# Strided scores of batch 1 in one half-array run, batch 0's strided x transposed before its last local scores: an attention and MLP kernel on one core

## The chip, the cores and the metric

The kernel runs on one core of a Trainium2 chip. The metric is the device time of one execution in microseconds. Five engines run beside each other, each through its own instruction list in order, and wait for each other through semaphores: TensorE (PE: matmuls and transposes; PEld is its loading of weights), VectorE (DVE), ScalarE (ACT), GpSimd (POOL) and SyncE (SP), which only issues DMA transfers here. Matmul results land in PSUM, eight banks of 2 KB per partition; VectorE and ScalarE copy them from there into SBUF.

## What is computed

```python
scores = scale * np.matmul(q, k.transpose(0, 1, 3, 2))          # B=8, H=8, S=576, D=64
mask_local = (rel >= 0) & (rel < 32)                            # heads 0 to 3
mask_strided = (rel >= 0) & (pos[None, :] % 32 == pos[:, None] % 32)   # heads 4 to 7
attn = softmax(np.where(masks, scores, -1e9))
x = (attn @ v).transpose(0, 2, 1, 3).reshape(B * S, H * D)      # 4608 x 512
h = x @ w_in                                                    # 512 -> 2048
out = (h * np.tanh(softplus(h))) @ w_out                        # 2048 -> 512
```

All inputs and the output are float32; the matmuls work in bf16.

## The kernel before

The 4608 rows of x are worked on in nine blocks of 512. For a block t there are two projections: `mlp1` (x times w_in, then Mish on ScalarE) and a second product (times w_out, then the store). Batch 1's attention is threaded into block 0's second product, batch 2's into block 1's, and so on. The order of all instructions is written out by hand; no scheduler changes it.

Strided attention (kind "s") of a batch is sixteen score tiles of 72x72, one for each of 4 heads and 4 pairs of residues; local attention (kind "l") is six windows of 96 queries and 128 keys for four heads. Both are cut into three parts ("s", 0) to ("s", 2) and ("l", 0) to ("l", 2). The steps are:

- `t_step` transposes a batch's q or k on PE (line 253 strided, line 267 local) and copies the result to qTs, kTs, qTl or kTl. The local transposes use 64 of the array's 128 columns.
- `qk` (line 333) computes one part's scores. Its contraction is over 64 rows, half of the array. An exp on ScalarE (line 347) follows. For batch 0 the mask is added before by `bias` (line 304); for later batches `mask` (line 353) multiplies the exps by 0 or 1.
- `pv` (line 369) multiplies the exps by v and a column of ones, and VectorE divides by the sum: a reciprocal and a multiplication (lines 380 and 381) into x_s or x_l. `pv2` (lines 394 and 395) does two at once. A step V of kind s, number i, is called "V s i" below, of kind l "V l i".
- `xt` transposes x_s (line 418) or x_l (line 408) and copies it into xT, the input of the first projection. `xt_now` and `xt_later` do the same for x_l window by window, the first on PE, the second by a transposing DMA in SyncE's queue.

Run here means a stretch of half-array matmuls with full-array matmuls before and after it. A half-array run is made either by `qk` or by a local `t_step`.

PSUM is handed out as three accumulators of two banks (`acc(i)`, i = 0 to 2, one buffer each) and two single banks that `tile_t` hands out in turn (the pool tag is "pt"). A new tile in a buffer waits until the last reader of the former tile is done.

Batch 0's attention (lines 904 to 958) stands before everything else: there is no projection yet to hide it. Its strided scores, local transposes, local scores, outputs and transposes of x are written one after another, then block 0's first projection. That projection's first three groups are split in two halves: `g1s` needs only the strided half of xT (four w_in matmuls a group, 128x512, line 522), the other halves also the local part.

Block 0's second product has sixteen steps of four matmuls (line 781, 128x512 each). Step i is followed by the list `at[i]` of batch 1's attention steps (`attn_steps`, the branch with x == y, lines 455 to 474) and by a few more that lines 966 to 977 append: loads for batch 2, sums of w_out's quarters (line 656) and the transposing DMAs for batch 2. The steps use w_out in four parts, each loaded by a DMA of its own; steps 8 to 11 need the third. After step 15 block 1 begins with line 553 (psu).

Of the kernel before, what the change touches and what calls it, by code (L numbers as in the profile page):

```python
# [11 lines left out]
BF16 = mybir.dt.bfloat16  # L12
# [5 lines left out]
WQ = 96  # L18
CL, PL = 6, 96
# [24 lines left out]
def kernel(ctx, tc, q, k, v, moe_w_in, moe_w_out, out):  # L44
    nc = tc.nc
    B, H, S, D = q.shape
# [87 lines left out]
    def by_head(x):  # L134

        return x[0:PL].rearrange("p j h d -> p (j h d)").rearrange("p (h x) -> p h x", h=4)
# [19 lines left out]
    def spread_v_str(b, eng):  # L156
        cast(eng, vs[b % 2][0:PN, :, :, 0:D], vs_raw().rearrange("p h (j d) -> p h j d", d=D))
# [37 lines left out]
    def cast(eng, out_, in_):  # L195
        if eng is nc.scalar:
            nc.scalar.copy(out_, in_)  # L197
        else:
            eng.tensor_copy(out_, in_)
# [42 lines left out]
            eng.memset(vl[b % 2][0:32, 0, :, 0:D], 0.0)  # L242


    def t_step(b, kind, which, hp, eng=None):

        eng = eng or nc.vector
        tr = tile_t("tr")[:].bitcast(BF16)
        if kind == "s":
            src = (qs if which == "q" else ks)[b % 2]  # L250
            for u in range(8):
                h, jj = 2 * hp + u // 4, u % 4
                nc.tensor.transpose(  # L253
                    tr[:, PN * u:PN * u + PN],
                    src[0:PN, h, 128 * jj:128 * jj + 128],
                    ident[0:PN, 0:PN],
                )
            dst = (qTs if which == "q" else kTs)[:, 8 * SU * hp:8 * SU * hp + 8 * SU]
            cast(
                eng, dst.rearrange("c (u n) -> c u n", u=8)[:, :, 0:PN],  # L260
                tr[:, 0:S].rearrange("c (u n) -> c u n", u=8),
            )
        else:
            src = by_head((ql if which == "q" else kl)[b % 2])
            for j in range(CL):
                for e in range(2):
                    nc.tensor.transpose(  # L267
                        tr[64 * e:64 * e + 64, PL * j:PL * j + PL],
                        src[:, 2 * hp + e, D * j:D * j + D], ident[0:PL, 0:PL],
                    )  # L270
            dst = qTl[:, hp, :] if which == "q" else kTl[:, hp, 32:32 + S]
            cast(
                eng, dst.rearrange("c (p j) -> c p j", j=CL),
                tr[:, 0:S].rearrange("c (j p) -> c p j", j=CL),
            )

    def unread(n, i_acc=None):

# [15 lines left out]
    class Attn:  # L294
# [129 lines left out]
                    tr[:, 0:576].rearrange("p (j n) -> p n j", j=CS),  # L424
                )

        def xt_now(self, n):
            tr = tile_t("trx")[:].bitcast(BF16)
            t0 = (self.b % RING) * S
            for c in range(2):  # L430
                for w in range(n):
                    o = (n * c + w) * WQ
                    nc.tensor.transpose(
                        tr[:, o:o + WQ], x_l[0:WQ, w, 128 * c:128 * c + 128], ident[0:WQ, 0:WQ]
                    )
            cast(
                nc.scalar, xT[:, 0:2, t0:t0 + n * WQ],
                tr[:, 0:2 * n * WQ].rearrange("p (c n) -> p c n", c=2),
            )

# [6 lines left out]
    def attn_steps(b, x, y):  # L447

        a = Attn(b)
        Q = lambda i_acc, *parts: (lambda: a.qk(parts, i_acc))  # L450
        M = lambda kd, i: (lambda: a.mask(kd, i, nc.vector))
        V = lambda kd, i: (lambda: a.pv(kd, i))
        X = lambda kd, hf: (lambda: a.xt(kd, hf))
        s0, s1, sl2, l0, l1 = ("s", 0), ("s", 1), (("s", 2), ("l", 2)), ("l", 0), ("l", 1)
        if x == y:
            T = [(lambda n=n, eng=eng: t_step(b, *T_ORDER[n], eng)) for n, eng in enumerate(
                (None, None, None, None, None, nc.scalar, None, nc.scalar))]
            return [
                T[2:4], [Q(x, s0)],
                [M(*s0), Q(x, s1)],  # L460
                [lambda: spread_v_str(b, nc.vector), V("s", 0)],
                [V("s", 1), M(*s1), Q(x, ("s", 2))],
                [V("s", 2), T[4]],
                [V("s", 3), M("s", 2), T[5]],
                [V("s", 4), T[6]],
                [V("s", 5), T[7]],
                [V("s", 6), Q(x, l0)],
                [V("s", 7), M(*l0), Q(x, l1)],
                [X("s", 0), V("l", 0), M(*l1), Q(x, ("l", 2))],
                [X("s", 1), V("l", 1), M("l", 2)],  # L470
                [V("l", 2), V("l", 3)],
                [V("l", 4), V("l", 5)],
                [lambda hf=hf: a.xt("l", hf, nc.vector) for hf in range(2)],
            ], T[0:2]
        V2 = lambda kd, i, z: (lambda: a.pv2(kd, i, z))
        G = lambda kd, i: (lambda: a.mask(kd, i, nc.gpsimd))
        l2 = ("l", 2)
        now = -(-(512 * (b + 1) - S * b) // WQ)
        at = [
            [],  # L480
            [Q(x, s0), Q(y, s1), Q("t", *sl2), M(*s0), M(*s1), M("s", 2)],
            [],
            [V2("s", 0, y), G(*l2)],
            [],
            [V2("s", 2, y), Q(x, l0), Q("t", l1), G(*l0), G(*l1)],
            [],
            [V2("s", 4, y), lambda: nc.scalar.preload_act_table(AF.Mish)],
            [],
            [V2("s", 6, y)],
            [V2("l", 0, x)],  # L490
            [X("s", 0), V2("l", 2, y), X("s", 1)],
            [V2("l", 4, x), lambda: a.xt_now(now)],
            [lambda: a.xt_later(now)],
        ]
        return at
# [180 lines left out]
    def sums_w():  # L676

        b11, b12 = w_out[:, 0:8, 0:256], w_out[:, 0:8, 256:512]
        b21, b22 = w_out[:, 8:16, 0:256], w_out[:, 8:16, 256:512]
        return [  # L680
            lambda c: sums(tw_of(0)[:, c], b12[:, c], b11[:, c], ALU.subtract),
            lambda c: sums(tw_of(1)[:, c], b22[:, c], tw_of(0)[:, c], ALU.subtract),
            lambda c: sums(b12[:, c], b22[:, c], b12[:, c], ALU.subtract),
            lambda c: sums(tw_of(3)[:, c], b21[:, c], tw_of(1)[:, c], ALU.subtract),
        ]
# [174 lines left out]
    with tc.manual_schedule():  # L860
# [56 lines left out]
            a.qk([("s", i)], None, ps[i])  # L917
        spread_v_str(0, Dv)
        unread(3)
        t_step(0, "l", "k", 0, Dv)  # L920
        t_step(0, "l", "k", 1, Sc)
        a.qk([("s", 2)], None, ps[2])
        a.pv2("s", 0, 0)
        a.pv2("s", 2, 1)
        for hp in range(2):
            t_step(0, "l", "q", hp, Sc)
# [2 lines left out]
        a.pv2("s", 6, 1)  # L929
        a.qk([("l", 0)], None, ps[0])  # L930
        a.qk([("l", 1)], None, a.bias("l", 1, 0))
        a.qk([("l", 2)], None, a.bias("l", 2, 2))
        load_w_out(0, 1)
        load_qk_str(1)
# [5 lines left out]
        load_v_loc(1)  # L940
        accs = (1, 0, 2)
        gT, g1s, g1 = mlp1(0, accs)
        a.pv2("l", 0, 1)
        a.xt("s", 0)
        a.xt("s", 1)
        a.pv2("l", 2, 0)
        a.pv2("l", 4, 2)
        g1s[0]()
        a.xt("l", 0)
        a.xt("l", 1)  # L950
        Sc.preload_act_table(AF.Mish)
        g1s[1]()
        g1s[2]()
        for f in sums_w_in()[0:3]:
            f()
# [5 lines left out]
        for t in range(NBLK):  # L961
            if t == 0:
                x, y, z = accs
                at, ts = attn_steps(1, y, y)
                at[3] += [
                    lambda: load_early_v_str(2), lambda: load_tiles_loc(2, kl, k),
                    lambda: cast_v_loc(1, Po), lambda: load_tiles_loc(2, ql, q),
                ]
                at[12].append(lambda: transpose_by_dma(2))
                at[1].append(lambda: sums_w()[0](lo))  # L970
                at[7].append(lambda: sums_w()[0](hi))
                at[9].append(lambda: sums_w()[1](lo))
                at[11].append(lambda: sums_w()[1](hi))
                at[14].append(lambda: sums_x(1, "1"))
                at[15] += [
                    lambda: spread_v_str(2, Dv),
                ]
                out_accs = (z, x)
            else:
                if t == 1:  # L980
                    split_third()
                x, y = 0, 1
                gT, z, g1 = mlp1(t, (y, x) if t == 1 else (x, y))
                at = attn_steps(t + 1, x, y) if t + 1 < B else []
                if t == 1:
                    at[0].append(lambda: sums_w()[3](hi))
                if t + 2 < B:
                    at[10].append(lambda: transpose_by_dma(t + 2))
                if t + 1 < B:
                    at[7].append(lambda: share_v_loc(t + 1))  # L990
                if t + 2 < B:
                    at[0].append(lambda: load_qk_str(t + 2))
                if t + 1 < B:
                    at[12].append(lambda: sums_x(t + 1, "1"))
# [55 lines left out]
```

## Time and profile before

| What | us |
|---|---|
| median of 3 runs (286.89 to 287.18) | 287.12 |
| the profiled execution | 286.68 |
| its span, first to last instruction | 284.8 |
| PE's first w_in matmul (line 522) | 19.91 |
| last of 64 w_in matmuls of block 0 starts | 34.46 |
| block 0's second product: first transpose of batch 1 | 34.67 |
| block 1's first matmul (line 553) | 57.39 |
| landing of w_out's four parts | 29.47, 38.03, 46.21, 49.91 |

The profile lists one execution. A timeline line gives the start of a group of equal instructions, its busy time, the engine, the line, what it writes and reads, the shape and the count; in brackets is the idle time of the engine before it and what ended that. PE's matmuls overlap each other, so a matmul's cost is read from start to start: 0.216 us for 512 columns, 0.032 for 72.

### The profile page before, as it was taken

How to read it: one execution, taken by the hardware profiler on the slowest of the kernel's cores; microseconds unless marked ns; L12 is line 12 of the kernel's file. 1: busy time of each engine (PE TensorE's matmuls, PEld its weight loads, DVE VectorE, ACT ScalarE, POOL GpSimd, SP SyncE). 2: the span in 40 equal slices, each digit the busy share in tenths (PEclk: the TensorE clock that was granted, in tenths of full speed). 3: DMA queues.
4: the chain of work that ended last, by engine and by line, in shares of the span. 5: the costliest groups of instructions: out<-in, count | busy, mean ns of one | idle time of the engine just before them, and what ended most of it. 6: DMA issues, size and time to landing. Idle time of an engine off the chain costs nothing.

```text
span 284.8 us, 7535 instructions
## 1 busy us (share of the span) xinstructions
PE 279.0 (98%) x3121; PEld 218.6 (77%) x3121; DVE 193.0 (68%) x403; ACT 196.4 (69%) x292; POOL 106.3 (37%) x127
## 2 busy tenths in 40 slices
PE   8999999999999999999999999999999999999995
PEld 3564455586898689868988898788978997888684
DVE  2283067899877777777777778777677767644742
ACT  1578652599867987798779877987699759407820
POOL 8375534406290717271636255345404600000000
PEclk9999999999999999999999999999999999999999
DMA  7999999999989999799999999899979041003004
GB/s 155 185 202 195 190 194 201 143 145 235 169 128 129 214 173 150 139 216 158 155 138 217 122 176 136 216 135 153 157 143 164 4 154 30 0 10 140 0 2 147
DMA packets 103965, 40.73 MB, mean 143 GB/s; under 512 B 86396, under 2 KB 99436, under 8 KB 103932
## 3 DMA queue, kind: packets, MB, share of 16 engines
q1 hardware_dynamic: 67900, 25.13, 51.9%
q0 software_dynamic: 35744, 14.87, 46.8%
q8 instruction: 24, 0.39, 0.6%
q10 hardware_dynamic: 288, 0.25, 0.3%
q14 instruction: 9, 0.07, 0.1%
HBM read 37.20 MB, written 9.44 MB: 164 GB/s over the span
## 4 chain that ended last, share of the span: by engine, by line
PE 92%; DMA 2%; DVE 2%; ACT 1%; issue 0%; ACTq 0%; POOLq 0%
PE pso L748 31%; PE psu L553 10%; PE psh L522 10%; PE psv L553 9%; PE psb L553 8%; PE psb L522 5%; PE po L369 4%; PE pso L808 4%; PE pso L781 4%; PE ps L333 4%; DMA ks<-in_k_dram 2%; PE trx L418 1%; PE un L281 1%; PE tr L267 1%; PE tr L253 1%; DVE x_s L395 1%
## 5 line engine op out<-in xcount | busy, mean ns | idle before, releaser
L748 PEld LDWEIGHTS <-gT 128*128 128x128 bf16 x448 | 41.9, 98 | 5.8
L553 PEld LDWEIGHTS <-w_in 128*128 128x128 bf16 x384 | 37.4, 98 | 8.4
L353 POOL TENSOR_TENSOR Pl<-Pl,consts_sb 128x960 bf16<-128x960 bf16 (+1 forms) x18 | 29.2, 1634 | 38.2 <-issue 22.1
L748 PE MATMUL pso<-w_out,gT 128*128 128x256 bf16 x336 | 40.9, 272 | 0.0
L748 PEld LDWEIGHTS <-Sg 128*128 128x128 bf16 x336 | 31.5, 98 | 4.4
L522 PEld LDWEIGHTS <-w_in 128*128 128x128 bf16 x208 | 20.2, 98 | 16.7 <-issue 0.6
L553 PEld LDWEIGHTS <-Sw 128*128 128x128 bf16 x288 | 28.2, 98 | 3.3
L522 PE MATMUL psh<-xT,w_in 128*128 128x512 bf16 (+1 forms) x136 | 29.4, 366 | 0.2 <-ACT xT L197 0.2
L197 ACT COPY xT<-trx 128x576 bf16<-128x576 bf16 (+3 forms) x24 | 14.2, 629 | 18.4 <-PE trx L418 13.0
L748 PE MATMUL pso<-Tw,Sg 128*128 128x256 bf16 x224 | 26.7, 273 | 0.0
L197 ACT COPY osb<-pso 128x512 f32<-128x512 f32 (+1 forms) x17 | 9.4, 555 | 20.2 <-PE pso L748 10.8
L562 ACT ACTIVATE gT<-psu 128x1024 bf16<-128x1024 f32 x16 | 16.4, 1025 | 8.4 <-PE psu L553 8.4
L395 DVE TENSOR_TENSOR x_s<-po,rden 72x512 bf16<-72x512 f32 x28 | 19.2, 686 | 1.0
L656 DVE TENSOR_TENSOR psu<-psb,p 128x512 f32<-128x512 f32 x16 | 11.2, 700 | 11.8 <-PE psb L553 11.0
L533 ACT ACTIVATE gT<-psh 128x1024 bf16<-128x1024 f32 x16 | 16.2, 1024 | 4.0 <-PE psh L522 3.9
L175 POOL DMA_DIRECT2D vl<-in_v_dram x24 | 17.8, 751 | 2.0 <-issue 1.5
L656 DVE TENSOR_TENSOR Sg<-gT 128x256 bf16<-128x256 bf16 (+2 forms) x32 | 12.8, 422 | 8.0 <-ACT gT L562 6.7
L628 POOL COPY mark<-qTl 1x4 bf16<-1x4 bf16 x6 | 1.6, 268 | 44.4 <-DMA qTl<-ql 44.4
L347 ACT ACTIVATE Ps<-ps 72x864 bf16<-72x864 f32 (+1 forms) x18 | 14.7, 857 | 4.6 <-PE ps L333 4.6
L553 PE MATMUL psu<-xT,w_in 128*128 128x256 bf16 x128 | 17.9, 272 | 0.0
L725 DVE TENSOR_TENSOR p<-pso,p 128x512 f32<-128x512 f32 x14 | 9.6, 685 | 11.9 <-PE pso L748 11.9
L553 PE MATMUL psb<-Sx,w_in 128*128 128x256 bf16 x128 | 17.2, 272 | 0.0
(139 smaller groups left out, 612.8 us busy)
## 6 DMA issues: line engine op xcount, KB each, us to landing
out_dram<-osb SPq DMA_DIRECT2D x9, 512.0 KB, 3.9
out_dram<-p SPq DMA_DIRECT2D x7, 512.0 KB, 3.0
kl<-in_k_dram SPq DMA_DIRECT2D x5, 576.0 KB, 13.6
ql<-in_q_dram SPq DMA_DIRECT2D x5, 576.0 KB, 16.4
qs<-in_q_dram POOLq DMA_DIRECT2D x8, 288.0 KB, 12.0
vsr<-in_v_dram POOLq DMA_DIRECT2D x8, 288.0 KB, 9.0
w_in<-in_moe_w_in_dram POOLq DMA_DIRECT2D x4, 512.0 KB, 9.8
w_out<-in_moe_w_out_dram POOLq DMA_DIRECT2D x4, 512.0 KB, 17.9
```

The source lines that it names most:

```text
L175: nc.gpsimd.dma_start(vl[b % 2][32:128, :, h, 0:D], v[b, h].rearrange("(w p) d -> p w d", p=WQ))
L197: nc.scalar.copy(out_, in_)
L333: nc.tensor.matmul(by_e[e][:, o:o + w], lhsT=lhsT, rhs=rhs, start=not biased, stop=True, skip_group_check=biased,)
L347: nc.scalar.activation(pt[0:n, :, 0:nw], ps[0:n, :, o0:o0 + nw], AF.Exp, scale=scale)
L353: meng.tensor_tensor(out=pm, in0=pm, in1=mk[0:n, :].unsqueeze(1).unsqueeze(1).to_broadcast([n, 2, nu, w]), op=ALU.mult,)
L395: nc.vector.tensor_tensor(out=dst.rearrange("p e (h d) -> p e h d", h=4), in0=po[0:m, :, :, 0:D], in1=rden[0:m].unsqueeze(3).to_broadcast( ...
L522: nc.tensor.matmul(ps_u[:, o:o + n], lhsT=w_in[:, cc, fc * 128:(fc + 1) * 128], rhs=xT[:, cc, a:a + n], start=(cc == 2 and (o == 0 or len( ...
L533: nc.scalar.activation(to, tiles[g][:], AF.Mish)
L553: nc.tensor.matmul(p[:, 256 * j:256 * j + 256], lhsT=lhs[:, cc, f:f + 128], rhs=rhs[:, cc], start=(first and j == 0 and cc == 0), stop=(la ...
L562: nc.scalar.activation(gT[:, c:c + src.shape[1], 256 * half_t:256 * half_t + 256], src, AF.Mish,)
L656: nc.vector.tensor_tensor(out=out_, in0=in0, in1=in1, op=op)
L748: nc.tensor.matmul(ps[:, pair, :], lhsT=lhs(c, 128 * pair), rhs=rhs(c), start=(first and pair == 0 and c == 0), stop=(last and c == 7), sk ...
```

## The change

Batch 0, before the first projection:

- `pv2("s", 0)` moves ahead of the two local transposes of k, and the first of those copies goes from VectorE to ScalarE.
- The strided x is transposed (`xt("s", 0)` and `xt("s", 1)`) before the last local scores, after the first two local parts' scores; its two copies go from ScalarE to VectorE.
- Local outputs 0 and 1 are made by two single `pv` (in the two single banks) instead of one `pv2`.
- The three strided halves of the first projection no longer stand together: the first one comes after these two outputs, the second one between the transposes of local x, the third one after them.

Batch 1, inside block 0's second product:

- The two strided score parts s0 and s1 are computed in one run after step 1; s1 uses the two single banks instead of the accumulator, so its exp comes as two instructions. The spread of v and both masks follow at once on VectorE.
- The four local transposes are made in two runs instead of four, k after step 5 and q after step 7. Each pair fills one accumulator; VectorE copies its first half, ScalarE its second.
- Local x is transposed by `xt_now(5)` with one VectorE copy, its sixth window by a transposing DMA.
- One sum of w_out's quarters comes one step earlier.

```diff
+    def t_loc(b, which, hp, tr):
+        src = by_head((ql if which == "q" else kl)[b % 2])
+        for j in range(CL):
+            for e in range(2):
+                nc.tensor.transpose(
+                    tr[64 * e:64 * e + 64, PL * j:PL * j + PL],
+                    src[:, 2 * hp + e, D * j:D * j + D], ident[0:PL, 0:PL],
+                )
+        dst = qTl[:, hp, :] if which == "q" else kTl[:, hp, 32:32 + S]
+        return lambda eng: cast(
+            eng, dst.rearrange("c (p j) -> c p j", j=CL),
+            tr[:, 0:S].rearrange("c (j p) -> c p j", j=CL),
+        )
...
         if x == y:
-            T = [(lambda n=n, eng=eng: t_step(b, *T_ORDER[n], eng)) for n, eng in enumerate(
-                (None, None, None, None, None, nc.scalar, None, nc.scalar))]
+            T = [(lambda n=n: t_step(b, *T_ORDER[n])) for n in range(4)]
+
+            def t_pair(which):
+                tr = acc(x, "tr")
+                copies = [t_loc(b, which, hp, tr[:, hp, :].bitcast(BF16)) for hp in range(2)]
+                for copy, eng in zip(copies, (nc.vector, nc.scalar)):
+                    copy(eng)
+
             return [
-                T[2:4], [Q(x, s0)],
-                [M(*s0), Q(x, s1)],
-                [lambda: spread_v_str(b, nc.vector), V("s", 0)],
-                [V("s", 1), M(*s1), Q(x, ("s", 2))],
-                [V("s", 2), T[4]],
-                [V("s", 3), M("s", 2), T[5]],
-                [V("s", 4), T[6]],
-                [V("s", 5), T[7]],
+                T[2:4],
+                [Q(x, s0), Q("t", s1), lambda: spread_v_str(b, nc.vector), M(*s0), M(*s1)],
+                [],
+                [V("s", 0)],
+                [V("s", 1), Q(x, ("s", 2))],
+                [V("s", 2), M("s", 2), lambda: t_pair("k")],
+                [V("s", 3)],
+                [V("s", 4), lambda: t_pair("q")],
+                [V("s", 5)],
                 [V("s", 6), Q(x, l0)],
                 [V("s", 7), M(*l0), Q(x, l1)],
                 [X("s", 0), V("l", 0), M(*l1), Q(x, ("l", 2))],
                 [X("s", 1), V("l", 1), M("l", 2)],
                 [V("l", 2), V("l", 3)],
                 [V("l", 4), V("l", 5)],
-                [lambda hf=hf: a.xt("l", hf, nc.vector) for hf in range(2)],
+                [lambda: a.xt_now(5, nc.vector), lambda: a.xt_later(5)],
             ], T[0:2]
...
         spread_v_str(0, Dv)
         unread(3)
-        t_step(0, "l", "k", 0, Dv)
+        a.pv2("s", 0, 0)
+        t_step(0, "l", "k", 0, Sc)
         t_step(0, "l", "k", 1, Sc)
         a.qk([("s", 2)], None, ps[2])
-        a.pv2("s", 0, 0)
         a.pv2("s", 2, 1)
...
         a.qk([("l", 1)], None, a.bias("l", 1, 0))
+        a.xt("s", 0, Dv)
+        a.xt("s", 1, Dv)
         a.qk([("l", 2)], None, a.bias("l", 2, 2))
...
-        a.pv2("l", 0, 1)
-        a.xt("s", 0)
-        a.xt("s", 1)
+        a.pv("l", 0)
+        a.pv("l", 1)
+        g1s[0]()
         a.pv2("l", 2, 0)
         a.pv2("l", 4, 2)
-        g1s[0]()
         a.xt("l", 0)
+        g1s[1]()
         a.xt("l", 1)
         Sc.preload_act_table(AF.Mish)
-        g1s[1]()
         g1s[2]()
...
-                at[1].append(lambda: sums_w()[0](lo))
+                at[0].append(lambda: sums_w()[0](lo))
```

More of the change, by code (lines that the diff above doesn't have):

```diff
@@ L263, in t_step @@
         else:
[L264 to L275, printed above, removed]
+            t_loc(b, which, hp, tr)(eng)
     def unread(n, i_acc=None):
@@ L425, in xt, with xt_now @@
                 )
-        def xt_now(self, n):
+        def xt_now(self, n, eng=nc.scalar):
             tr = tile_t("trx")[:].bitcast(BF16)
@@ L436, in xt_now @@
             cast(
-                nc.scalar, xT[:, 0:2, t0:t0 + n * WQ],
+                eng, xT[:, 0:2, t0:t0 + n * WQ],
                 tr[:, 0:2 * n * WQ].rearrange("p (c n) -> p c n", c=2),
```

## The prediction

> **What bounds the kernel now.** I read the busy times first, then TensorE's waits, then the timeline of the two stretches that the diff touches.
>
> ```profile
> PE 279.0 (98%) x3121; PEld 218.6 (77%) x3121; DVE 193.0 (68%) x403; ACT 196.4 (69%) x292; POOL 106.3 (37%) x127
> ```
>
> TensorE (PE) is busy for 98% of the span, so an edit counts only by what it does to PE's start times. From 57.39 us, where block 1 begins, the matmuls stand back to back, and PE's list of waits names nothing there: whatever happens earlier shifts the end by the same amount. So I need two numbers: when PE starts the thirteenth w_in matmul (end of the prologue), and how long PE takes from there to 57.39.
>
> The prologue, in the timeline (start, duration, engine, line, tiles, count, idle before and who ended it):
>
> ```profile
> 13.47 0.76 DVE L199 COPY kTl<-tr 128x576 bf16<-128x576 bf16 x1 [1.18 <-PE tr L267]
> 13.73 0.64 ACT L197 COPY kTl<-tr 128x576 bf16<-128x576 bf16 x1
> ...
> 14.26 0.65 ACT L347 ACTIVATE Ps<-ps 72x576 bf16<-72x576 f32 x1
> ...
> 15.04 1.18 ACT L197 COPY qTl<-tr 128x576 bf16<-128x576 bf16 x2
> ...
> 17.03 0.58 PE L304 MATMUL ps<-consts_sb 128*128 128x480 bf16 x2 [0.16 <-DVE x_s L395]
> ...
> 18.85 0.20 DVE L394 RECIPROCAL rden<-po 96x8 f32<-96x8 f32 x1 [1.04 <-PE po L369]
> ...
> 20.44 0.81 PE L522 MATMUL psh<-xT,w_in 128*128 128x512 bf16 x3 [0.15 <-ACT xT L197]
> ...
> 21.72 8.58 PE L522 MATMUL psh<-xT,w_in 128*128 128x512 bf16 x39
> ```
>
> To see: PE waits for VectorE's x_s (17.03) and ScalarE's xT copies (20.44); VectorE stands idle for 1.04 us before the local outputs. From 21.72 PE runs without a gap, four w_in matmuls already done.
>
> Block 0's second product, where batch 1's attention is threaded in:
>
> ```profile
> 36.58 1.03 PE L781 MATMUL pso<-w_out,gT 128*128 128x512 bf16 x4
> ...
> 37.54 0.37 PE L333 MATMUL ps<-qTs,kTs 64*128 64x72 bf16 x12
> ...
> 37.84 1.04 PE L781 MATMUL pso<-w_out,gT 128*128 128x512 bf16 x4
> ...
> 38.95 0.37 PE L333 MATMUL ps<-qTs,kTs 64*128 64x72 bf16 x12
> ...
> 46.25 1.02 PE L781 MATMUL pso<-w_out,gT 128*128 128x512 bf16 x4
> ```
>
> To see: what a half-array run (64 rows here, 64 columns for the transposes) costs. Four 512-wide matmuls are followed by a full-array group after 0.87 us (35.19 to 36.06), by a half-array one after 0.96 (36.58 to 37.54): 0.10 to enter. Twelve half-array matmuls at 16 ns should take 0.19 us, and the next group comes after 0.30: 0.11 to leave. **A run costs 0.21 us** besides its matmuls.
>
> **Part 1, the prologue.** Hand-over times, from rows: PE's last start to a reader's start 0.24 us; ScalarE's end to PE 0.05, VectorE's 0.06; a ScalarE copy follows its neighbour after 0.54 (two in 1.18); an s pair of reciprocal and multiply takes 0.92 on VectorE. I follow the new order.
>
> ScalarE gets both k copies. pv2 s0 now leads and needs the first exp (12.15 + 0.89 = 13.04): 13.10 to 13.33 on PE. The k transposes start at 13.45, so the copies run 13.94 to 15.11 and the s2 exp 15.01 to 15.66 (before: 14.91). The q copies end at 16.74 (before: 16.22).
>
> The l0 bias goes into the accumulator that the s2 exp reads, so it waits until 15.71 (before 15.19), and in PE's queue pv2 s4 stands behind it: 16.13 (before 15.60). VectorE finishes s0 and s2 early (15.71), then idles 0.87 and does s4 until 17.51 and s6 until 18.40 (before 16.97 and 17.81). The l1 bias waits for s4: 17.57 (before 17.03); l1's scores end at 18.26, and the sixteen moved x_s transposes run 18.39 to 18.88 (0.0323 each).
>
> Their two copies are now VectorE's. The trace has no VectorE copy of this form, a read from PSUM with stride 72. The bounds are 0.46 us (VectorE's xT copies of local x, contiguous, two in 0.82 at 57.33) and 0.76 (the kTl copy at 13.47, stride 96). I take 0.75, the strided row: 18.86 to 20.28. [...]
>
> Both copies hold the two banks of the pool "pt", from which pv l0 and pv l1 now draw. Pv l1 therefore waits for the second copy: 20.36 (before, the first local outputs ran at 18.38). Behind it in PE's queue stand the first four w_in matmuls, 20.49 to 21.35, then pv2 l2 to 21.59 and l4. VectorE does l0 and l1 (0.62 each) until 21.49, l2 until 22.74, l4 until 23.64 (before: all by 21.44). The transposes of windows 0 to 2 finish at 22.94, four w_in matmuls to 23.85, the other transposes to 24.06, four more to 24.96; ScalarE's last xT copy ends at 24.94. **The thirteenth w_in matmul starts at 24.99; before, 21.72 + 8 × 0.216 = 23.45: 1.54 us later.** With copies of 0.46 the same chain gives 24.40: 0.95 later.
>
> **Part 2, block 0's second product,** on the clock of before. It took 34.67 to 57.39, 22.72 us. Removed: three runs, 3 × 0.21 = 0.62; two of twelve transposes of 42 ns, 0.08. Waits of PE that showed as late starts, 0.90 in all: s1's scores behind s0's exp on one accumulator (0.14 at 38.95); V s0 behind VectorE's spread of v (0.07); V s2 behind the s1 mask (0.14); the load of w_out (0.07 at 46.25); l1's scores behind l0's exp (0.10); V l2 to V l5 behind VectorE (0.38). s1's scores now use the pool's banks, and spread and masks come two steps earlier, so the first three go; the fourth goes because PE comes later than the landing at 46.21. **What is late next is VectorE:** from V l0 at 51.04 it has pairs, masks and a w_out sum without a break, 3.72 us to V l3's end as before (52.10 to 55.82); V l3 and V l5 wait for banks, 0.07 and 0.26, l1's scores 0.10. So 0.47 of the waits goes. Following every step, block 1 begins at 56.24 on that clock: **1.14 us saved** (the terms add up to 1.17).
>
> Costed at nothing: the w_out sum one step earlier (0.68 at 37.26, in VectorE's 0.99 of idleness before the mask); s1's exp in two halves of 72x432 (a 128x384 took 0.50, a 72x576 0.65; their mask is needed a whole step later); the pair copies, where ScalarE's waits for VectorE's in the built order (done at 44.7 and 47.1, read from 45.0 and 47.7; if that 0.3 were overrun, PE waits for the excess); VectorE's xT copy of 960 (0.46 to 0.92, done by 57.4, needed at 58.5). Window 5 goes by one transposing DMA in SyncE's queue, behind block 0's two stores and ahead of batch 3's local loads (issued at 65.30, landed 73.62 and 83.21). At 1.2 us of issue and 5.6 to landing it is there by 73; block 2 reads it after 86, the casts of the loads come after 100. POOL's order is unchanged.
>
> **Sum:** 1.54 − 1.14 = +0.40 us. The profiled execution took 286.68 us, of which 284.8 are the span and 1.9 lie around it; it becomes 287.08. It lay 0.44 below the median of 287.12, so I forecast **287.5 us**, +0.14%. About 0.2% (0.57 us) is what a measurement of this kernel can tell from no change.
>
> **Rivals.** (A, slower) VectorE takes back what the dropped runs give. Place: steps 11 to 15 of the second product, where V l2 to V l5 share two banks and VectorE has no idle time left. Price: the 0.52 us of waits and transposes are not saved, only the runs' 0.62: +0.92, 288.0. It decides as soon as VectorE reaches V l0 0.17 us later than I have it. For it: V l4 and V l5 already waited; against: VectorE reaches V l0 with 0.6 us of idleness in the trace. Chance 0.32. (B) Strided copies at the contiguous price: +0.95 − 1.14 = −0.2, 286.9, no measurable change. Against: both strided kTl copies in block 0 took 0.74. Chance 0.10. (C, faster) The prologue loses nothing, because the early transposes remove PE's 0.54 us of waiting for xT and the chain above does not bind. Then the third w_out load caps the gain: step 8 cannot start before its landing at 46.21, and only 11.13 − 10.59 = 0.54 is saved behind it (from 46.25 to 57.39 before, from 45.65 to 56.24 after): 286.6, or 286.5 if the load lands a little earlier. For it: PE's late starts in that stretch, 1.35 us in all (0.10 at 14.55, 0.28 inside the sixteen po matmuls from 15.60, 0.23 at 17.03, 0.07 at 17.93, 0.54 from 19.9 to 20.7, 0.13 inside the transposes from 21.09); against: both banks and VectorE. Chance 0.09. That the change does not do what it says is ruled out by the built order: seven runs stand there.
>
> **How the numbers follow.** Forecast 0.49, A 0.32, B 0.10, C 0.09. The forecast, B and the tamer end of C (0.02) lie within 0.2%, 0.61; slower is A, 0.32; faster the rest of C, 0.07. The range 286.8 to 288.1 takes in both copy prices (286.9 and 287.5) and A's 288.0; what is left out is C and the far side of A.
>
> **What would show it.** In the new timeline: VectorE's two xT copies of about 0.75 from 18.9; pv l1 near 20.4; the thirteenth w_in matmul near 25.0; three half-array runs fewer between there and block 1; step 8 starting past 47 without a DMA wait; block 1 at 57.8. I am wrong if ScalarE's k copies do not push the s2 exp past 15.5, if the copies take 0.46, or if V l0 to V l5 show more than 0.5 us of waits on PE.

## The result

The changed kernel takes 287.49 us (median of 22 runs, 287.25 to 288.73); the kernel before takes 286.91 us in the same series (median of 22, 286.64 to 287.52). The ratio is 1.002 with a 95% interval from 1.0014 to 1.0026: slower by 0.58 us, or 0.20%, just at the bound up to which I called it no change. Forecast was a change of +0.40 us. The profiled executions took 286.68 us (span 284.8) and 287.36 us (span 285.5).

For all that follows I cut the span into pieces that do not depend on when the inputs land. That landing differs from execution to execution: the first exp started between 12.15 and 12.89 us in the kernels measured here. The pieces are: first exp to last w_in matmul of block 0 (the prologue), from there to block 1's first matmul (the second product of block 0), and block 5, from its first matmul to block 6's.

| Piece, us | before | after | difference | forecast |
|---|---|---|---|---|
| first exp to last w_in matmul | 22.31 | 23.78 | +1.47 | +1.54 |
| last w_in matmul to block 1 | 22.93 | 21.78 | −1.15 | −1.14 |
| block 5 | 28.89 | 29.25 | +0.35 | 0 |

The other blocks agree within 0.05. The sum is +0.67, and the two profiled executions differ by 0.68. The medians differ by 0.1 less: before's profiled execution was shorter than its median (286.68 against 286.91), with inputs that landed early.

**The prologue.** First the busy times on the page of the changed kernel, then its timeline (start, duration, engine, line, tiles, shape, count, idle before and who ended it). Lines from 245 on have moved, by 3 for `qk`, `bias` and `pv`.

```profile
PE 277.5 (97%) x3104; PEld 218.4 (76%) x3119; DVE 194.2 (68%) x405; ACT 195.9 (69%) x292; POOL 106.9 (37%) x127
```

```profile
13.95 1.18 ACT L197 COPY kTl<-tr 128x576 bf16<-128x576 bf16 x2
...
15.01 0.65 ACT L350 ACTIVATE Ps<-ps 72x576 bf16<-72x576 f32 x1
...
17.55 0.58 PE L307 MATMUL ps<-consts_sb 128*128 128x480 bf16 x2 [0.42 <-DVE x_s L398]
...
18.85 1.42 DVE L199 COPY xT<-trx 128x576 bf16<-128x576 bf16 x2 [0.52 <-PE trx L421]
...
20.32 0.29 PE L372 MATMUL po<-vl,Pl 128*128 128x65 bf16 x4 [0.36 <-DVE xT L199]
...
21.77 0.20 DVE L397 RECIPROCAL rden<-po 96x8 f32<-96x8 f32 x1 [0.42 <-PE po L372]
...
22.76 0.34 PE L411 MATMUL trx<-consts_sb,x_l 96*128 96x96 bf16 x4 [0.68 <-DVE x_l L398]
```

Read against the lines of before: the s2 exp has gone from 14.26 to 15.01, behind two k copies on ScalarE; the second bias from 17.03 to 17.55, still behind VectorE's x_s; the strided copies stand on VectorE from 18.85; single output l1 waits for the second of them and starts at 20.32; and the transposes of x_l wait for VectorE until 22.76, where before they ended at 21.68. The w_in matmuls run without a break from 24.06, four of them after eight earlier ones, so the thirteenth comes at 24.92 (forecast 24.99; 23.45 before).

**The second product,** in the timeline of PE:

```profile
39.04 0.56 PE L336 MATMUL ps<-qTs,kTs 64*128 64x72 bf16 x24
...
43.80 0.70 PE L249 MATMUL tr<-consts_sb,Sg 96*64 96x96 bf16 x24
...
46.52 0.70 PE L249 MATMUL tr<-consts_sb,Sg 96*64 96x96 bf16 x24
47.15 1.04 PE L791 MATMUL pso<-w_out,gT 128*128 128x512 bf16 x4
...
57.31 0.59 PE L436 MATMUL trx<-consts_sb,x_l 96*128 96x96 bf16 x10
57.73 0.49 PE L563 MATMUL psu<-xT,w_in 128*128 128x256 bf16 x3
```

To see: s0 and s1 are one run of 24; k and q one run of 24 each; step 8 starts at 47.15 with no wait for a DMA (the third part of w_out landed at 46.23); block 1 begins at 57.73, forecast 57.8.

**Block 5** is where the forecast had nothing. The changed kernel's list of PE's waits (who waited for whom: us in total, times, longest) has a line that the list of before has not:

```profile
PE psb L563 <- DVE psu L666: 0.3, 1, 0.3
```

And the timeline of VectorE there, in the kernel before and in the changed one:

```profile
176.80 1.50 DVE L656 TENSOR_TENSOR psu<-psb,p 128x512 f32<-128x512 f32 x2 [0.24 <-PE psb L553]
```

```profile
177.17 0.70 DVE L666 TENSOR_TENSOR psu<-psb,p 128x512 f32<-128x512 f32 x1 [1.07 <-PE psb L563]
178.32 0.70 DVE L666 TENSOR_TENSOR psu<-psb,p 128x512 f32<-128x512 f32 x1 [0.46 <-PE psb L563]
```

Before, the two sums follow each other (the second 0.104 us after the first, as in every other block). In the changed kernel the second one starts 0.455 after it, though the matmuls that it is said to wait for had their last start at 177.66, 0.66 earlier; such sums otherwise start about 0.3 us after it (177.29 and 177.60 before). PE's next matmuls wait for this sum. I come to the cause below.

### The profile page after: what moved, and what is told of

Read it like the earlier page. It is cut to its first block, busy times and chain, and to the rows that moved or that the text cites. A ratio compares the mean times of both kernels' runs of the same rounds, so it can differ in the third digit from the quotient of the medians.

```text
span 285.5 us, 7520 instructions
## 1 busy us (share of the span) xinstructions
PE 277.5 (97%) x3104; PEld 218.4 (76%) x3119; DVE 194.2 (68%) x405; ACT 195.9 (69%) x292; POOL 106.9 (37%) x127
## 4 chain that ended last, share of the span: by engine, by line
PE 94%; DVE 3%; ACT 1%; issue 1%
PE pso L758 30%; PE psu L563 10%; PE psh L532 10%; PE psv L563 8%; PE psb L563 7%; PE psb L532 5%; PE po L372 5%; PE pso L818 4%; PE pso L791 4%; PE ps L336 3%; PE un L284 3%; PE trx L421 1%; PE tr L267 1%; PE ps L307 1%; PE trx L436 1%
## 5 line engine op out<-in xcount | busy, mean ns | idle before, releaser
L532 PE MATMUL psh<-xT,w_in 128*128 128x512 bf16 (+1 forms) x127 | 28.8, 366 | 0.5
L197 ACT COPY xT<-trx 128x576 bf16<-128x576 bf16 (+3 forms) x22 | 13.1, 626 | 20.9 <-PE trx L421 13.0
L350 ACT ACTIVATE Ps<-ps 72x864 bf16<-72x864 f32 (+1 forms) x17 | 13.8, 854 | 4.2 <-PE ps L336 4.2
```

The costliest lines, as they stand in the source:

```text
L350: nc.scalar.activation(pt[0:n, :, 0:nw], ps[0:n, :, o0:o0 + nw], AF.Exp, scale=scale)
L532: nc.tensor.matmul(ps_u[:, o:o + n], lhsT=w_in[:, cc, fc * 128:(fc + 1) * 128], rhs=xT[:, cc, a:a + n], start=(cc == 2 and (o == 0 or len( ...
```

## The experiments

My theory was the forecast's: two terms, each a chain worked out by hand, which add; and w_out's landing as a cap on what batch 1's part gains without batch 0's. The rivals were that the parts do not stand by themselves, that the prologue's loss has other causes than those named, and that block 5's loss belongs to one of the parts.

The results are together in this table. The pieces are those of above, in us of the profiled execution. The ratio is to the kernel before, which was measured again beside the experiments: its median was 286.96 beside batch1_only, batch0_only, pair_in_acc and k_copy_on_vector, 286.97 beside the next four rows, 286.90 beside batch1_quarters and early_xt_timed, and 286.61 (one execution) beside xt_on_scalar and early_xt_only. Differences to before are taken to these. The row early_xt is one kernel in two runs: early_xt_only, one execution of 286.14, and early_xt_timed, whose median stands there.

| Kernel | prologue | second product | block 5 | median | ratio, 95% interval |
|---|---|---|---|---|---|
| before | 22.31 | 22.93 | 28.89 | 286.91 | |
| after | 23.78 | 21.78 | 29.25 | 287.49 | 1.0020 (1.0014 to 1.0026) |
| batch1_only | 22.32 | 22.48 | 28.93 | 286.28 | 0.9978 (0.9967 to 0.9988) |
| batch0_only | 23.78 | 22.89 | 29.24 | 288.68 | 1.0062 (1.0050 to 1.0074) |
| pair_in_acc | 23.22 | 21.78 | 28.89 | 286.66 | 0.9989 (0.9980 to 0.9997) |
| k_copy_on_vector | 23.22 | 21.78 | 28.89 | 286.55 | 0.9989 (0.9980 to 0.9998) |
| after_plus_one | 23.78 | 21.78 | 28.89 | 287.32 | 1.0010 (1.0001 to 1.0019) |
| before_plus_three | 22.51 | 22.88 | 29.25 | 287.48 | 1.0011 (1.0000 to 1.0022) |
| run_added | 23.78 | 22.36 | 29.25 | 288.07 | 1.0044 (1.0027 to 1.0061) |
| batch1_halves | 22.32 | 22.04 | 28.89 | 286.01 | 0.9962 (0.9950 to 0.9975) |
| early_xt | 22.65 | 21.78 | 28.89 | 286.08 | 0.9968 (0.9954 to 0.9981) |
| xt_on_scalar | 24.04 | 21.78 | 28.89 | 287.62 (one run) | |
| batch1_quarters | 22.31 | 22.58 | 28.89 | 285.82 | 0.9959 (0.9947 to 0.9972) |

### Each part by itself

Batch 1's part alone is the changed kernel with before's lines from `spread_v_str(0, Dv)` to `g1s[2]()`. Batch 0's part alone is the changed kernel with before's `attn_steps` branch and w_out sum.

> Batch 1's part of the change alone, on the prologue of before. My theory (two terms that add, the second one capped): the second product begins at 34.67 as before; the dropped runs and waits would bring step 8 to 47.15 - 1.50 = 45.65, but it waits for the third part of w_out (46.21 before, 46.23 after) until about 46.25. The rest takes 10.58 as in the changed kernel (57.73 - 47.15), so block 1 begins at 56.8, 0.55 earlier than before, and the time is 0.55 below that of before (about 286.4). Rival 1, no cap: block 1 at 56.2, time 1.15 lower (285.8). Rival 2, the batch 1 part is what costs 0.35 us in block 5 (first projection 173.8 to 203.0 took 29.25 in the changed kernel, 28.89 before): block 5 stays 29.25 long and only 0.2 is gained.

> Batch 0's part alone, on the second product of before. My theory: the last w_in matmul of block 0 starts at 35.95 as in the changed kernel (34.46 before), +1.50; the second product is that of before without the 0.07 wait for w_out, so block 1 begins at 58.8 (57.39 + 1.50 - 0.07) and the time is 1.4 above that of before, 288.3. Rival: the 0.35 us of block 5 come from this part, then block 5 takes 29.25 and the time is 1.8 above, 288.7. If the two parts alone gave the same sum as together (+0.58), this one would have to be +1.7 with -1.15 of the other, or +1.1 with -0.55.

Batch 1's part alone gains 0.68 us in the medians, not 1.15 (0.55 was expected); in the pieces of the profiled execution its second product is 0.45 shorter. PE's timeline of that kernel shows why:

```profile
45.24 0.70 PE L249 MATMUL tr<-consts_sb,Sg 96*64 96x96 bf16 x24
46.58 1.02 PE L791 MATMUL pso<-w_out,gT 128*128 128x512 bf16 x3 [0.64 <-DMA w_out<-in_moe_w_out_dram]
```

Step 8 was due at 45.95 and waited for the third part of w_out, which landed at 46.54. From step 8 on to block 1 it took 10.58 us, the same as in the changed kernel, as expected. The cap is shown, and rivals 1 and 2 are out.

Batch 0's part alone costs 1.72 us, where my theory had 1.4 and the rival 1.8. The prologue is as expected (23.78, the same as in the changed kernel to 0.01), but block 5 is 0.35 longer here too. So this loss goes with batch 0's part. Block 5 begins over 130 us after that part has ended, which made me look for something other than a delay that is handed on.

### Block 5: a place in VectorE's instruction list

I counted the instructions in VectorE's program, waits on semaphores included, from zero. The late sum is number 320 in the changed kernel and in batch 0's part alone. It is 317 in the kernel before and in batch 1's part alone, and 318 and 321 in the two kernels below; none of these showed the gap. To test this I moved the number and nothing else, with tiny instructions where VectorE has time:

```diff
+        for _ in range(1):            # 1 in the changed kernel, 3 in the kernel before
+            Dv.memset(x_s[0:1, 0, 0:4], 0.0)
```

> The changed kernel with one more tiny VectorE instruction (a memset of four elements, written over later) among the memsets at the start. In the changed kernel and in batch 0's part alone VectorE began the second sum of block 5's second product 0.455 us after the sum before it, everywhere else 0.104 after; that instruction is number 320 in VectorE's program in these two kernels, and 317, 317, 318 and 321 in the four others measured (before and batch 1's part alone are both 317). Theory: the 0.35 us hang on the place of the instruction in VectorE's program. Then here (number 321) the gap is 0.104, block 5 takes 28.89 instead of 29.25, and the time is 0.35 below the changed kernel's: about 287.1, 0.2 above before. Rival: they hang on the time at which block 5 starts (173.8 and 175.0 in these two, 173.2 to 173.4 in the others) or on which transfers then run: the gap stays 0.455, time 287.5.

> The kernel before with three more such memsets at the start: its second sum of block 5 becomes number 320 in VectorE's program. Theory of the place: the gap there becomes 0.455, block 5 takes 29.25 instead of 28.89, time 0.35 above before. Rival (start time of block 5, or the transfers then running): nothing changes, 0.00, since block 5 starts at 173.4 as before.

VectorE's timeline in block 5, with one more instruction in the changed kernel, and then with three more in the kernel before:

```profile
177.37 1.50 DVE L666 TENSOR_TENSOR psu<-psb,p 128x512 f32<-128x512 f32 x2 [0.87 <-PE psb L563]
```

```profile
177.71 0.70 DVE L656 TENSOR_TENSOR psu<-psb,p 128x512 f32<-128x512 f32 x1 [0.63 <-PE psb L553]
178.86 0.70 DVE L656 TENSOR_TENSOR psu<-psb,p 128x512 f32<-128x512 f32 x1 [0.46 <-PE psb L553]
```

The gap went from the one and came to the other: block 5 takes 28.89 with 321 and 29.25 with 320. The start of the block does not decide: the changed kernel (start at 173.79) has the gap, the one with an instruction more (173.99) has not, the one of before with three more (174.33) has it again. The ratios moved the same way, to 1.0010 from 1.0020 and to 1.0011 from 1. The interval of the kernel with three more begins at 1.0000, and its profiled execution had a prologue 0.20 longer, for a reason that was not followed: there the trace decides, not the time. So about half of what the changed kernel loses against before is this (0.0010 of 0.0020 by the ratios, 0.35 of 0.67 us by the pieces), and it has nothing to do with what the change computes. It happened that the change makes VectorE's list three instructions longer ahead of block 5.

### The prologue's loss taken apart

Two undoings, one by one and then together. The first puts the lines around the local k transposes back; the second puts local outputs 0 and 1 into an accumulator:

```diff
-        a.pv2("s", 0, 0)
-        t_step(0, "l", "k", 0, Sc)
+        t_step(0, "l", "k", 0, Dv)
         t_step(0, "l", "k", 1, Sc)
         a.qk([("s", 2)], None, ps[2])
+        a.pv2("s", 0, 0)
```

```diff
-        a.pv("l", 0)
-        a.pv("l", 1)
-        g1s[0]()
+        a.pv2("l", 0, 1)
         a.pv2("l", 2, 0)
         a.pv2("l", 4, 2)
+        g1s[0]()
```

> The changed kernel with the lines around the local k transposes as before (first copy on VectorE, strided outputs 0 behind them). My theory (the second k copy on ScalarE delays everything behind the s2 exp by 0.52): s2 exp at 14.26, q copies end at 16.22, l0 bias 15.19, VectorE's x_s s6 until 17.81, l1 bias 17.03, xT copies 18.33 to 19.75, last w_in matmul at 35.43 instead of 35.95, block 1 at 57.2, time 0.52 below the changed kernel's, 287.0. Rival: the 0.52 us that VectorE idles ahead of its xT copies (18.33 to 18.85) absorb it, and nothing moves at the last w_in matmul: 35.95, 287.5.

> The changed kernel with local outputs 0 and 1 in accumulator 1 (one pv2, as before) and the first strided half of the projection behind all the outputs; the early transposes of x and their VectorE copies stay. My theory (the two banks that the copies hold, and the single outputs behind them, cost the largest part of the prologue's loss): the outputs run from 19.26 on, VectorE does l0 to 21.08, l2 to 21.91, l4 to 22.74 (22.70 and 23.54 for l2 and l4 in the changed kernel); the thirteenth w_in matmul at 24.3, 0.63 earlier, the last one at 35.3; step 8 at 46.5, still past the landing of w_out at 46.2; block 1 at 57.1, time 286.9, the same as before. Rival: the copies on VectorE and the later scores set the chain and the banks do not matter: last w_in matmul still within 0.1 of 35.95, time 287.5.

> Both undoings of the prologue together (k copies as before; local outputs 0 and 1 in accumulator 1, first strided half behind the outputs): of batch 0's part only the earlier transposes of strided x with their VectorE copies stay, and the place of the second strided half. Measured from the first exp to the last w_in matmul of block 0, to leave out when the inputs land: before 22.31, changed kernel 23.78, each undoing by itself 23.22. Theory: the three causes stand one behind the other in VectorE's chain and add: 23.78 - 0.56 - 0.57 = 22.65, so that the early transposes by themselves still cost 0.34. Step by step: VectorE's copies 18.33 to 19.75 and its outputs l0, l2, l4 until 20.56, 21.39, 22.22 (21.44 before), thirteenth w_in matmul at about 23.8. Rival: the early transposes cost nothing by themselves (they take PE's former wait of 0.54 for xT): 22.3 or less.

Each undoing by itself takes 0.56 or 0.57 us from the prologue (expected 0.52 and 0.63), and both together 1.13, to 22.65 as expected. In time the two single ones gained 0.94 and 0.83, not 0.52 and 0.63: both also move VectorE's instruction off number 320. So the +1.47 splits into 0.56 for the lines around the local k transposes (both copies on ScalarE, strided outputs 0 ahead of them; these two were not undone one by one, but the s2 exp stands behind the second copy in the timeline), 0.57 for the single outputs in the two banks with the w_in matmuls behind them, and 0.34 for what is left: the early transposes with their copies on VectorE, and the place of the second strided half. That the early transposes cost nothing because they free PE of its wait for xT, rival C of the forecast, is refuted: VectorE's outputs come later, and that is what PE waits for instead, as its list of waits says for the kernel with both undoings:

```profile
PE psh L532 <- DVE rden L397: 0.8, 1, 0.8
```

In that kernel VectorE has no gap from the copies to the last local output:

```profile
18.43 1.42 DVE L199 COPY xT<-trx 128x576 bf16<-128x576 bf16 x2 [0.53 <-PE trx L421]
19.77 0.19 DVE L397 RECIPROCAL rden<-po 96x8 f32<-96x8 f32 x1
20.00 0.69 DVE L398 TENSOR_TENSOR x_l<-po,rden 96x512 bf16<-96x512 f32 x1
20.61 0.19 DVE L397 RECIPROCAL rden<-po 96x8 f32<-96x8 f32 x1
20.83 0.69 DVE L398 TENSOR_TENSOR x_l<-po,rden 96x512 bf16<-96x512 f32 x1
21.44 0.19 DVE L397 RECIPROCAL rden<-po 96x8 f32<-96x8 f32 x1
21.67 0.69 DVE L398 TENSOR_TENSOR x_l<-po,rden 96x512 bf16<-96x512 f32 x1
```

Would the copies have been better left on ScalarE? The edit is `a.xt("s", hf)` for `a.xt("s", hf, Dv)`.

> The changed kernel with the two copies of strided x on ScalarE, as before, at their new place. Theory (the banks are what holds the single outputs, whichever engine copies): ScalarE takes the copies behind the l1 exp, 19.46 to 20.6, single output 1 starts at about 20.7 instead of 20.4, VectorE reaches l2 0.1 later; from the first exp to the last w_in matmul 23.9 (changed kernel 23.78). Rival (VectorE's 1.42 us of copies are the loss, since it has the outputs to do): 0.3 or more less, 23.5.

No: 24.04, 0.26 worse than the changed kernel, where 0.1 was expected. ScalarE has the l1 exp ahead of the copies (they ran 19.44 to 20.62), VectorE idles for 2.06 us, and output l1 still waits for the bank. PE's list of waits in that kernel names it:

```profile
PE po L372 <- ACT xT L197: 0.9, 2, 0.6
```

So it is the banks that hold the single outputs, whichever engine empties them.

### What a run costs

The pair of k transposes in two runs, each with its copy at once:

```diff
+            def t_half(which, hp):
+                if hp == 0:
+                    half[which] = acc(x, "tr")
+                copy = t_loc(b, which, hp, half[which][:, hp, :].bitcast(BF16))
+                copy((nc.vector, nc.scalar)[hp])
...
-                [V("s", 2), M("s", 2), lambda: t_pair("k")],
-                [V("s", 3)],
+                [V("s", 2), M("s", 2), lambda: t_half("k", 0)],
+                [V("s", 3), lambda: t_half("k", 1)],
```

> The changed kernel with the pair of k transposes in two runs: the first after step 5, the second after step 6, each copied at once, first on VectorE, second on ScalarE. Eight half-array runs instead of seven. Theory (a run costs 0.21 us to enter and leave): from the last w_in matmul of block 0 to block 1 it takes 21.78 + 0.21 = 21.99, and block 1 begins 0.21 later; the time is 0.2 above the changed kernel's. Rival (what the change saved there is the waits and VectorE's order, a run by itself costs nothing beyond its matmuls): 21.78, no difference; or VectorE is the bound to block 1 and absorbs the run: less than 0.1.

The second product takes 0.58 longer, not 0.21. The timeline of PE:

```profile
44.14 0.45 PE L249 MATMUL tr<-consts_sb,Sg 96*64 96x96 bf16 x12
44.52 1.04 PE L799 MATMUL pso<-w_out,gT 128*128 128x512 bf16 x4
45.39 0.29 PE L372 MATMUL po<-vs,Ps 72*128 72x65 bf16 x4
45.97 0.45 PE L249 MATMUL tr<-consts_sb,Sg 96*64 96x96 bf16 x12 [0.29 <-DVE kTl L199]
```

The second half waits for VectorE's copy of the first, because both halves lie in one accumulator. It starts 0.484 us after the last of V s3's matmuls, where the pair in one run starts 0.123 after V s2's: 0.36 of wait that I had not thought of. What is left, 0.58 − 0.36 = 0.22, is the run, as costed from the rows of before. My experiment measured the run only after this subtraction; a version without the wait was not tried.

### Lifting the cap

Batch 1's part alone, with w_out's third part loaded in two transfers, and then in four (the kernel with two writes the same loop in another form):

```diff
-        for c in range(c0, c1):
+        for c in range(c0, c1):
+            n = 2 if c == 2 else 4        # 1 in the second kernel
+            for f in range(4 * c, 4 * c + 4, n):
                 nc.gpsimd.dma_start(
-                    w_out[:, 4 * c:4 * c + 4, :],
-                    moe_w_out.rearrange("(fc p) o -> p fc o", p=128)[:, 4 * c:4 * c + 4, :],
+                    w_out[:, f:f + n, :],
+                    moe_w_out.rearrange("(fc p) o -> p fc o", p=128)[:, f:f + n, :],
                 )
```

> Batch 1's part alone, with the third part of w_out loaded by two transfers of half the size. With one transfer, step 8 had its turn at 45.95 and waited for the landing at 46.54 until 46.58. Theory (that wait alone caps the gain): the first half lands about 1.5 us earlier (the part before it landed at 43.15, so the halves come at about 44.9 and 46.5); step 8 begins at 45.95 with two matmuls, and the third waits until 46.58: 0.43 of the 0.63 us is gained, block 1 at 56.7, time 0.43 below batch 1's part alone, 285.85. Rival 1: the smaller transfers move later or share the engines, both halves land at 46.5: no gain. Rival 2: VectorE and POOL are the next bound (the cast of v for batch 1 ended at 50.9, its first output began at 51.6): gain below 0.2.

> Batch 1's part alone, with the third part of w_out in four transfers. With two halves the landings were 44.93 and 46.61 and step 8's third matmul still waited 0.3. Theory: the quarters land about 0.85 us apart, at 44.1, 44.9, 45.8 and 46.6, against their use at 45.95, 46.16, 46.38 and 46.60; no wait of PE is left in step 8, and from the last w_in matmul to block 1 it takes 21.78 as in the changed kernel (two halves: 22.04): time 0.2 to 0.3 below the halves', 285.7 to 285.8. Rival: smaller transfers are slower and land later: 22.04 or more.

> The kernel of the run with both undoings of the prologue, timed. Its profile had block 1 at 56.74, no wait for w_out (its prologue is 0.34 longer than that of before, so step 8 comes at 46.16), and no 0.35 us in block 5. By the parts: 0.34 - 1.15 = -0.81 against before, of which its profiled run showed 0.64 at block 1, with inputs that landed 0.17 later. Expected 286.2, 0.8 below before. If the landing of w_out binds in most executions (it came at 45.8 to 46.6 in the runs so far), 0.2 to 0.4 less than that.

The halves landed at 44.93 and 46.61, and PE's timeline shows step 8 broken in two as expected:

```profile
45.95 0.39 PE L793 MATMUL pso<-w_out,gT 128*128 128x512 bf16 x1
46.65 0.59 PE L793 MATMUL pso<-w_out,gT 128*128 128x512 bf16 x2 [0.32 <-DMA w_out<-in_moe_w_out_dram]
```

The second product takes 22.04 instead of 22.48, 0.44 less (expected 0.43); in the medians it is 0.27. The quarters landed at 43.88, 44.75, 45.59 and 46.46, and the wait for w_out is down to one of 0.08 inside step 8. But in the profiled execution another wait took its place, on the list of PE's waits:

```profile
PE po L374 <- POOL vl L244: 0.6, 1, 0.6
```

Batch 1's local v landed at 48.88 there (46.5 to 48.4 in the changed kernel and the two parts alone), POOL's cast of it was late by as much, and V l0 waited; so the second product took 22.58, not the 21.78 that was expected. Its load was also issued 0.7 us later than in batch 1's part alone (24.55 against 23.87); whether the four transfers do that was not tested. This is rival 2 of the halves, one step later. The median of five, 285.82, is nevertheless the lowest of all, 0.19 below the halves, and its profiled execution (286.31) the slowest of the five; the intervals of the two overlap, so I do not claim that four transfers beat two. The kernel with both undoings of the prologue, timed in a second run, took 286.08: 0.82 below before, expected 0.8. All of these beat both kernels; the best, at 0.9959, keeps the prologue of before.

## Why the prediction was right, and where it was not

**Prologue, +1.54 forecast, +1.47 measured.** Right, and link by link: s2 exp 15.01 (forecast 15.01), l1 bias 17.55 (17.57), first xT copy 18.85 (18.86), output l1 20.32 (20.36), transposes of windows 0 to 2 done 22.94 (22.94), thirteenth w_in matmul 24.92 (24.99). The VectorE copies took 0.76 and 0.75, the strided bound and not the contiguous one, so rival B is out. The experiments show the three groups of causes of the prologue's loss as separate terms (0.56, 0.57 and 0.34).

**Second product, −1.14 forecast, −1.15 measured.** Right in sum, and in its parts where these could be tested: the run at 0.22 (0.21), l1's scores 0.10 late, V l3 0.07 and V l5 0.25, against 0.10, 0.07 and 0.26. Rival A, VectorE taking back what the runs give, did not come: those waits are what the forecast had left in. ScalarE's pair copies did wait for VectorE's (they start at 45.61 and 48.11), and window 5 went by DMA; PE's list of waits names none of what was costed at nothing. VectorE's xT copy of 960 took 0.66.

**The step that failed** is in the first paragraph: "whatever happens earlier shifts the end by the same amount". A change can also shift which instruction stands at a certain place of an engine's list, and block 5 became 0.35 longer by that. Against the parts' sum of +0.32 (1.47 − 1.15) this is the larger term, and without it (changed kernel plus one instruction) the ratio is 1.0010. No wait of PE in the trace of before points to it.

**The time**, 287.5 against 287.49, agrees this closely by luck. I started from the median of three runs, 287.12; that of the 22 is 286.91. The base was 0.21 too high and the change 0.18 too low, and these cancel.

**The cap** (rival C's price) was right as a mechanism: as soon as the prologue loses nothing, w_out's landing binds. It came at 45.8 to 47.0 in the profiled executions, so it is a moving bound. Seen from the experiments, the two parts of the change do not add: batch 0's part delays step 8 past the landing, and only thereby does batch 1's part show its full 1.15. By itself it is worth 0.68 in the medians.

## What to carry to other kernels

Price a saving up to the next thing that it meets: here three dropped runs and fewer waits were worth 1.15 us on paper and 0.68 in fact, until the load behind them was cut into smaller transfers. Moving copies to an idle engine ahead of its critical work, and new tiles into banks that those copies hold, cost the whole chain behind them here (0.56 us together with the strided outputs put ahead, and 0.57 together with the w_in matmuls put behind the single outputs), though ScalarE and VectorE were busy for only 69% and 68% of the span. When two versions differ by a few tenths of a microsecond, put a dummy instruction into each before believing the difference: the place of one instruction in an engine's list was worth 0.35 us.

## What the runs showed of the hardware that I had not expected

An instruction at number 320 of VectorE's program started 0.35 us late in all four kernels where a sum that PE waits for stood there (after, batch0_only, before_plus_three, run_added), and the sum was on time in all other kernels measured, where its number was another. ScalarE has a like case: in the kernel with its copies of strided x on ScalarE, the copy of psu at 146.59 is number 192 in ScalarE's program; it started after 0.62 us of idleness, where the same copy in the changed kernel, number 190, started after 0.34. Block 4 took 29.21 there, 28.94 in the changed kernel. These are the lines of ScalarE's timeline in the changed kernel and in that one:

```profile
145.98 1.06 ACT L588 COPY psb<-psu 128x512 f32<-128x512 f32 x2 [0.34 <-PE psu L563]
```

```profile
146.59 1.06 ACT L588 COPY psb<-psu 128x512 f32<-128x512 f32 x2 [0.62 <-PE psu L563]
```

Both numbers are multiples of 64.

The traces hold two more things. First, number 448 of VectorE is late too. The sum into p at about 251 us has that number in four kernels (batch1_halves, batch1_quarters, pair_in_acc, xt_on_scalar), and there the profile shows VectorE idle for 3.77 to 3.79 us before it; in the ten other traces, where its number is 447 or 449 to 451, it was idle for 3.42. These are its lines in the kernel before (447) and in pair_in_acc (448):

```profile
251.13 0.69 DVE L725 TENSOR_TENSOR p<-pso,p 128x512 f32<-128x512 f32 x1 [3.42 <-PE pso L748]
```

```profile
251.35 0.69 DVE L735 TENSOR_TENSOR p<-pso,p 128x512 f32<-128x512 f32 x1 [3.77 <-PE pso L758]
```

PE does not wait for that sum, and no block is longer by it. Second, the records of DMA packets have packets of 8 KB in a queue of the kind "instruction" (q14). In all fourteen traces one of them starts 0.5 to 1.2 us after number 320 of VectorE, late or not. After number 448 one starts within 1.0 us in those four kernels, and in the kernel before and batch 1's part alone, where a wait for a semaphore has the number; in the other eight traces, where nothing is late at 448, the last one had come 3 to 8 us before. Each such packet starts after the late instruction has begun, so that instruction did not wait for that packet; what these packets carry and what makes the delay are not shown by any run. Numbers 320 and 448 lie 128 apart on one engine. The delay was 0.35 us at number 320 of VectorE and 0.28 (0.62 − 0.34) at number 192 of ScalarE.
